# Expert and attention kernel: early weight loads into later homes, and key features summed on VectorE

## The chip, the cores and the metric

The kernel runs on one core of a Trainium2 chip. A core has five engines that each follow a queue of their own: TensorE (PE; its weight loads are listed as PEld), VectorE (DVE), ScalarE (ACT), GpSimd (POOL) and SyncE (SP), which here issues DMAs. The metric is the device time of one execution in microseconds (us). Three runs of the kernel before were timed.

## The reference

Three stages follow one another: linear attention over 4 batches of 576 tokens and 8 heads, a gated product of four weight matrices, and a routing to one of 8 experts for each token.

```
def phi(x):
    proj = einsum('bhsd,df->bhsf', x, w_phi)             # 64 -> 128 features
    proj = proj - max(abs(proj), axis=-1, keepdims=True)
    return concatenate([exp(proj), exp(-proj)], axis=-1)
q_p, k_p = phi(q), phi(k)
kv  = einsum('bhsf,bhsd->bhfd', k_p, v)
z   = sum(k_p, axis=2)                                  # key features, summed over a batch's tokens
num = einsum('bhsf,bhfd->bhsd', q_p, kv)
den = einsum('bhsf,bhf->bhs', q_p, z)[..., None] + 1e-06
x   = (num / den), heads side by side                    # 2304 x 512
x   = ((x @ w1) * (x @ w2) @ w3) @ w_out                 # 512 -> 1024 -> 1024 -> 512, float64 weights
...
out[mask] = gate_w[mask, None] * (relu(x[mask] @ ew1[e]) @ ew2[e])   # for each expert e
```

The weights w1, w2, w3 and w_out of the middle stage arrive as float64, and are turned into float32 on the chip.

## The kernel before, in words

**Precision.** Most products run in three passes on a split of each operand into a high and a low part (mm3: high by high, high by low, low by high; lines 118 to 120). The split is a copy of the high part (line 102 on ScalarE, 104 on VectorE) and a subtraction (line 110, on VectorE or GpSimd). Products on plain float32 operands ("native") show two records for each instruction.

**Start of the program.** The start stage runs from the first load to the first product with w1 (tile pab). It does two things side by side. One is batch 0 of the attention. The other is the preparation of the weights: 40 blocks of 512 KB of float64 (8 of w_out, 8 of w1, 8 of w2, 16 of w3) are loaded as integers (tile raw, three buffers, line 207, 235 or 277) and converted by three VectorE instructions (lines 130, 132, 134, in f64_to_f32; the result is y, or wo for w_out). A block of w1 or w2 is then split into w1h and w1l, or w2h and w2l (ScalarE, and GpSimd for the low part). A block of w_out is transposed (tile pt), copied to woT and multiplied with the expert embeddings (tile pl); when all 8 are done, the last columns of wo are filled in (wo_c). Two blocks of w3 make one of 8 column blocks of W' = w3 @ w_out: 8 products each (tile pw, line 283), then a split of the two PSUM tiles into wph and wpl. PSUM gives 3 banks to pw, pab and px (tag pm) and 5 to the attention and the w_out work (tag pa).

**Attention.** Key and query tiles are 128 tokens by 4 heads (a group g; two groups make the 8 heads). A batch has 576 tokens, four whole tiles and a half one, which two batches share; so a batch is five pieces in each group. For one key piece the unit phi loads the tile (qkraw) and the values (v, two buffers), makes the projection (pphi), the largest absolute value (mx, line 325, VectorE) and eight exponentials on ScalarE into two tiles kf (lines 338 and 339; three buffers). The unit kv then issues four products with the values (kv, line 373) and four with a tile of ones, 32 columns wide (kz, line 377), which gives the sum z. After the fifth piece both PSUM tiles are copied (kvs), transposed (pkv, pkz) and split into ch and cl by the unit fin. The query units transpose pt (pqt), take exponentials (F, Hh, Ll), multiply (po), and divide (den, xf).

**Order of the work.** TensorE executes in the order in which the program is written; the other engines follow an order chosen by a scheduler when the program is built. Each attention unit has a due time on an axis of its own (LEAD_K, KEY_T, FIN_K, GAP_K are offsets on it), and attend(t) writes all units that are due before t. In the start stage attend is called after each piece of the weight work; after that, the units stand between those of the main loop: nine blocks of 256 tokens with 8 units pab (24 products each) and 4 units px, whose order follows the due times too. Batches 1 to 3 run there. The experts follow.

Of the kernel before, what the change touches and what calls it, by code (L numbers as in the profile page):

```python
# [23 lines left out]
NF = 128  # L24
# [28 lines left out]
GAP_K = 1.5  # L53
START_T = 32.0
START_P = 0.7
# [9 lines left out]
FIN_K = 0.3  # L65
# [27 lines left out]
class Kern:  # L93
# [103 lines left out]
    def load_w12(self, sp, w1, w2, wt):  # L197

        nc = self.nc
        out = []  # L200
        for src, name in ((w1, "w1"), (w2, "w2")):
            for kc in range(4):
                for u in range(2):
                    def go(src=src, name=name, kc=kc, u=u):
                        raw = sp.tile([P, 1, 512], I64, tag="raw64", name="raw64", bufs=RAW64)
                        c = slice(u * 512, (u + 1) * 512)
# [4 lines left out]
                    out.append(go)  # L211
        return out

    def build_w(self, sp, pp, app, w3t, w_out, wph, wpl):

# [5 lines left out]
        wo = sp.tile([P, 8, 2, HB], F32, name="wo")  # L221
# [47 lines left out]
        flat = [(0.5, u) for us in units for u in us]  # L269
        for fc in range(8):  # L270
            pss = []
            for half in range(2):
                def w_unit(fc=fc, half=half, pss=pss):
                    if half == 0:
                        pss.extend(pp.tile([P, 512], F32, tag="pm", name="pw") for _ in range(2))
                    raw = sp.tile([P, 4, P], I64, tag="raw64", name="raw64", bufs=RAW64)
                    nc.sync.dma_start(out=raw, in_=w3t[half * 512:(half + 1) * 512, fc * P:(fc + 1) * P]
                                      .rearrange("(a p) f -> p a f", p=P))
                    y = self.f64_to_f32(sp, raw, [P, 4, P])
                    for u in range(2):  # L280
                        for j in range(4):
# [914 lines left out]
```

## Time and profile before

| what | us |
|---|---|
| runs | 876.34, 878.03 and 1616.35, median 878.03 |
| the profiled execution | 877.96 |
| its span, from first to last instruction | 876.2 |
| TensorE busy, share of the span | 830.4, 95% |
| VectorE busy, share | 489.5, 56% |
| ScalarE busy, share | 400.7, 46% |
| GpSimd busy, share | 238.4, 27% |

The profiled execution took 877.96 us, within 0.1 us of the median, and its span leaves 1.76 us around it. A share of busy time is an average over stages; TensorE's matmuls overlap, and their ends are modelled, so the distance between starts tells more than the length of one.

### The profile page before, as it was taken

How to read it: one execution, taken by the hardware profiler on the slowest of the kernel's cores; microseconds unless marked ns; L12 is line 12 of the kernel's file. 1: busy time of each engine (PE TensorE's matmuls, PEld its weight loads, DVE VectorE, ACT ScalarE, POOL GpSimd, SP SyncE). 2: the span in 40 equal slices, each digit the busy share in tenths (PEclk: the TensorE clock that was granted, in tenths of full speed). 3: DMA queues.
4: the chain of work that ended last, by engine and by line, in shares of the span. 5: the costliest groups of instructions: out<-in, count | busy, mean ns of one | idle time of the engine just before them, and what ended most of it. 6: DMA issues, size and time to landing. Idle time of an engine off the chain costs nothing. (4 is left out here: it accounts for less than half of the span.)

```text
span 876.2 us, 15821 instructions
## 1 busy us (share of the span) xinstructions
PE 830.4 (95%) x5986; PEld 738.0 (84%) x5986; DVE 489.5 (56%) x1130; ACT 400.7 (46%) x1073; POOL 238.4 (27%) x257
## 2 busy tenths in 40 slices
PE   6899868999999999999999999979999999999996
PEld 4577657987899987899877999979998898988974
DVE  5788896653479844588543795443475362432200
ACT  5543335455576557475555763313243452433211
POOL 1122344321255312254212542130013301201010
PEclk9999988999999999999999999999999999999999
DMA  6677532002101011111011000032316641522410
GB/s 208 223 225 220 161 109 76 19 25 66 50 26 43 14 56 49 50 37 32 25 55 44 25 25 1 26 98 79 85 38 211 193 145 43 186 91 76 166 41 15
DMA packets 63536, 73.45 MB, mean 84 GB/s; under 512 B 7832, under 2 KB 50072, under 8 KB 63458
## 3 DMA queue, kind: packets, MB, share of 16 engines
q1 hardware_dynamic: 59618, 62.68, 23.1%
q0 software_dynamic: 3680, 9.72, 3.2%
q8 instruction: 48, 0.79, 0.4%
q14 instruction: 30, 0.25, 0.1%
q10 hardware_dynamic: 160, 0.02, 0.0%
HBM read 61.71 MB, written 10.95 MB: 83 GB/s over the span
## 5 line engine op out<-in xcount | busy, mean ns | idle before, releaser
L110 POOL TENSOR_TENSOR Ll<-F,Hh 128x512 fp32r<-128x512 f32 (+1 forms) x64 | 93.3, 1457 | 107.5 <-ACT Hh L102 101.2
L118 PE MATMUL px<-wph,abh 128*128 128x260 f32 x288 | 83.4, 290 | 5.0 <-DVE abh L104 5.0
L118 PE MATMUL pab<-xh,w1h 128*128 128x256 f32 x288 | 84.9, 295 | 0.1
L120 PE MATMUL pab<-xh,w1l 128*128 128x256 f32 x288 | 82.4, 286 | 0.0
L119 PE MATMUL pab<-xl,w1h 128*128 128x256 f32 x288 | 82.3, 286 | 0.0
L118 PE MATMUL pab<-xh,w2h 128*128 128x256 f32 x288 | 82.2, 285 | 0.0
L119 PE MATMUL pab<-xl,w2h 128*128 128x256 f32 x288 | 82.1, 285 | 0.0
L120 PE MATMUL px<-wph,abl 128*128 128x260 f32 x288 | 82.1, 285 | 0.0
L119 PE MATMUL px<-wpl,abh 128*128 128x260 f32 x288 | 82.1, 285 | 0.0
L120 PE MATMUL pab<-xh,w2l 128*128 128x256 f32 x288 | 82.0, 285 | 0.0
L567 DVE TENSOR_TENSOR ab<-pab,a 128x256 f32<-128x256 f32 x72 | 30.5, 423 | 89.5 <-ACT a L565 89.1
L119 PE MATMUL ph<-xsl,wth 128*128 128x256 f32 (+1 forms) x256 | 75.7, 296 | 0.5 <-DVE xsl L110 0.5
L118 PE MATMUL ph<-xsh,wth 128*128 128x256 f32 (+1 forms) x256 | 75.9, 296 | 0.3 <-ACT xsh L102 0.3
L120 PE MATMUL ph<-xsh,wtl 128*128 128x256 f32 (+1 forms) x256 | 75.5, 295 | 0.0
L565 ACT COPY a<-pab 128x256 f32<-128x256 f32 x72 | 27.0, 375 | 103.1 <-PE pab L120 87.7
L522 DVE RECIPROCAL den<-den 128x256 f32<-128x256 f32 (+1 forms) x32 | 62.3, 1948 | 16.2 <-ACT den L517 16.2
L283 PE MATMUL pw<-wo,y 128*128 128x260 f32 x256 | 62.7, 399 | 8.9 <-DVE wpl L110 7.5
L110 POOL TENSOR_TENSOR qkl<-qkraw,qkh 128x256 fp32r<-128x256 f32 x52 | 38.5, 743 | 114.9 <-ACT qkh L102 97.2
L283 PEld LDWEIGHTS pw<-wo,y 128*128 128x128 f32 x256 | 49.8, 199 | 19.2 <-DVE wpl L110 8.7
L901 DVE SCALAR_TENSOR_TENSOR hh<-ph,hh 128x256 fp32r<-128x256 f32 (+1 forms) x96 | 31.1, 353 | 58.0 <-ACT hh L897 49.5
L118 PEld LDWEIGHTS px<-wph,abh 128*128 128x128 f32 x288 | 55.0, 191 | 8.8 <-DVE abh L104 5.5
L829 POOL DMA_INDIRECT out_dram<-ob,ids x20 | 20.5, 1026 | 139.0 <-ACT ob L919 118.8
(220 smaller groups left out, 2390.6 us busy)
## 6 DMA issues: line engine op xcount, KB each, us to landing
wraw<-in_moe_w_dram SPq DMA_DIRECT2D x32, 512.0 KB
raw<-in_moe_w_dram SPq DMA_DIRECT2D x16, 512.0 KB
raw<-in_moe_w3t_dram SPq DMA_DIRECT2D x16, 512.0 KB
v<-in_v_dram SPq DMA_DIRECT2D x40, 128.0 KB
qkraw<-in_kT_dram SPq DMA_DIRECT2D x36, 128.0 KB
qkraw<-in_qT_dram SPq DMA_DIRECT2D x36, 128.0 KB
x2d<-x SPq DMA_DIRECT2D x18, 256.0 KB
raw<-in_moe_w_out_dram SPq DMA_DIRECT2D x8, 512.0 KB
```

Source lines behind the costliest of these rows:

```text
L110: e.tensor_tensor(out=out, in0=a, in1=b, op=ALU.subtract)
L118: nc.tensor.matmul(out, lhsT=lh, rhs=rh, start=start, stop=False)
L119: nc.tensor.matmul(out, lhsT=lh, rhs=rl, start=False, stop=False)
L120: nc.tensor.matmul(out, lhsT=ll, rhs=rh, start=False, stop=stop)
L283: nc.tensor.matmul(pss[u][:, :HB], lhsT=y[:, j, :], rhs=wo[:, jc, u, :], start=jc == 0, stop=jc == 7)
L522: nc.vector.reciprocal(den[:, :n], den[:, :n])
L565: nc.scalar.copy(a, ps[:, :BLK])
L567: nc.vector.tensor_tensor(out=ab, in0=ps[:, BLK:], in1=a, op=ALU.mult)
L829: self.nc.gpsimd.indirect_dma_start(out=out, out_offset=IndirectOffsetOnAxis(ap=ids[:m, i, 0:1], axis=0), in_=ob[:m, :], in_offset=None, b ...
L901: nc.vector.scalar_tensor_tensor(out=lo(h, i, j), in0=x, scalar=0.0, in1=h[:, i:j].bitcast(F32), op0=ALU.max, op1=ALU.subtract)
```

## The change

**Loads.** The raw blocks of w_out and w1 no longer go through the three buffers of raw. Each has a place of its own (tiles rwo and rw): in the memory that w2h, w2l, wph and wpl take later. Their loads are issued ahead, in pairs of w_out and w1, five ahead of the work (LOOK). w2 and w3 still go through raw, with each load issued three units ahead. All 8 blocks of w1 are converted beside the 8 of w_out; then come 8 groups of one block of w2 and two of w3. Attention units up to time 14 (START_K) stand in the first part, the rest up to 32 in the second; before, a power of the weight work's share set this.

**Key sums.** The first whole piece of a group writes its features into two tiles kacc (KACC = 2 buffers, so one group's worth). The other four pieces are added to them by VectorE, two instructions each, on 64 partitions for a half piece. The four products with ones run once a group, on kacc (unit sums, SUM_K after the last piece), so kz holds a PSUM bank only then. fin comes later (FIN_K), and a gap after a batch's keys is longer (GAP_K). kv_split writes ch and cl in four smaller splits for each pair of heads in place of two.

```diff
@@ -50,9 +50,10 @@
-GAP_K = 1.5
+GAP_K = 2.0
-START_P = 0.7
+START_K = 14.0
+LOOK = 5
-FIN_K = 0.3
+FIN_K = 1.0
+SUM_K = 0.1
+KACC = 2
...
-    def load_w12(self, sp, w1, w2, wt):
+    def early_raw(self, base, w1, w_out):
+        self.raw_wo, self.raw_w1, loads = [], [], [[], []]
+        for x, tag, n, name, dst in ((w_out, "w2h", 4 * DM, "rwo0", self.raw_wo), (w_out, "w2l", 4 * DM, "rwo1", self.raw_wo),
+                                     (w1, "wph", 4 * (BLK + 4) * 2, "rw10", self.raw_w1),
+                                     (w1, "wpl", 4 * (BLK + 4) * 2, "rw11", self.raw_w1)):
+            t = base.tile([P, n], I64, tag=tag, name=name, bufs=1)
+            for a in range(4):
+                i = len(dst)
+                raw = t[:, a * 512:(a + 1) * 512]
+                r, c = (i, slice(0, DM)) if x is w_out else (i // 2, slice((i % 2) * 512, (i % 2 + 1) * 512))
+                dst.append(raw.rearrange("p (a b) -> p a b", a=1))
+                loads[x is w1].append(lambda raw=raw, x=x, r=r, c=c:
+                                      nc.sync.dma_start(out=raw, in_=x[r * P:(r + 1) * P, c]))
+        return [x for pair in zip(*loads) for x in pair]
+
+    def conv_w1(self, sp, i, wt):
+        y = self.f64_to_f32(sp, self.raw_w1[i], [P, 1, 512])
+        c = slice((i % 2) * 512, (i % 2 + 1) * 512)
+        self.split(wt["w1h"][:, i // 2, c], wt["w1l"][:, i // 2, c], y[:, 0, :], WHI, WLO)
+
+    def late_w(self, sp, pp, base, w2, w3t, wt):
...
-        for src, name in ((w1, "w1"), (w2, "w2")):
-                    def go(src=src, name=name, kc=kc, u=u):
-                        nc.sync.dma_start(out=raw[:, 0, :], in_=src[kc * P:(kc + 1) * P, c])
-                        y = self.f64_to_f32(sp, raw, [P, 1, 512])
-                        self.split(wt[name + "h"][:, kc, c], wt[name + "l"][:, kc, c], y[:, 0, :], WHI, WLO)
...
+            def load():
+                st["r"] = sp.tile(shape, I64, tag="raw64", name="raw64", bufs=RAW64)
+                nc.sync.dma_start(out=st["r"] if shape[1] > 1 else st["r"][:, 0, :], in_=src)
+
+            out.append((load, lambda: unit(self.f64_to_f32(sp, st["r"], shape))))
...
+        def w2_unit(y, i):
+            if i == 0:
+                for n in ("w2h", "w2l"):
+                    wt[n] = base.tile([P, 4, DF], F32R, tag=n, name=n, bufs=1)
...
+            if fc == 0:
+                wp[:] = [base.tile([P, 8, 2, HB], F32R, tag=n, name=n, bufs=1) for n in ("wph", "wpl")]
+            for u in range(2):
+                self.split(wp[0][:, fc, u, :], wp[1][:, fc, u, :], pss[u][:, :HB], "a", "v")
+        for fc in range(8):
+            piece(w2[fc // 2 * P:(fc // 2 + 1) * P, (fc % 2) * 512:(fc % 2 + 1) * 512], [P, 1, 512],
+                  lambda y, fc=fc: w2_unit(y, fc))
+            for half in range(2):
+                piece(w3t[half * 512:(half + 1) * 512, fc * P:(fc + 1) * P].rearrange("(a p) f -> p a f", p=P), [P, 4, P],
+                      lambda y, fc=fc, half=half: w_unit(y, fc, half))
...
-                raw = sp.tile([P, 1, DM], I64, tag="raw64", name="raw64", bufs=RAW64)
-                nc.sync.dma_start(out=raw[:, 0, :], in_=w_out[jc * P:(jc + 1) * P, :])
+                raw = self.raw_wo[jc]
...
-            kf = ap.tile([P, 2, 256], F32, tag="kfk" if keep else "kf", name="kf", bufs=4 if keep else KB_)
+            tag, bufs = kind
+            kf = ap.tile([P, 2, 256], F32, tag=tag, name=tag, bufs=bufs)
...
+    def key_sums(self, zp, acc):
-            self.nc.tensor.matmul(out(zp, 32 * h, 32, 0), lhsT=self.one32[r0:r1, :],
-                                  rhs=kfs[h // 2][r0:r1, :, (h % 2) * NF:(h % 2 + 1) * NF], start=first, stop=last)
+            self.nc.tensor.matmul(zp[32 * h:32 * h + 32, 0:256].rearrange("p (s f) -> p s f", s=2), lhsT=self.one32,
+                                  rhs=acc[h // 2][:, :, (h % 2) * NF:(h % 2 + 1) * NF], start=True, stop=True)
...
-        so = pz[:, :256].rearrange("p (s h x) -> p h s x", h=4, x=32)[:, 2 * r:2 * r + 2, :, 0:1]
-        so = so.to_broadcast([P, 2, 2, D])
-        self.split(val(ch), val(cl), sv, CHI[self.ph], CLO[self.ph])
-        self.split(one(ch), one(cl), so, CHI[self.ph], CLO[self.ph])
+        so = pz[:, :256].rearrange("p (s h x) -> p h s x", h=4, x=32)
+        for c in range(2):
+            h, l = (x[:, c * 256:(c + 1) * 256].rearrange("p (s y d) -> p s y d", s=2, y=2) for x in (ch, cl))
+            self.split(h[:, :, c, :], l[:, :, c, :], sv[:, c], CHI[self.ph], CLO[self.ph])
+            self.split(h[:, :, 1 - c, :], l[:, :, 1 - c, :], so[:, 2 * r + c, :, 0:1].to_broadcast([P, 2, D]),
+                       CHI[self.ph], CLO[self.ph])
...
-                    st["f"] = self.key_feats(*self.phi_tile("k", t, g), keep)
+
+                    kind = ("kfk", 4) if keep else ("kacc", KACC) if n == whole else ("kf", KB_)
...
-                        kvp[:] = [self.app.tile([P, 512], F32, tag="pa", name=x) for x in ("kv", "kz")]
+                        kvp[0] = self.app.tile([P, 512], F32, tag="pa", name="kv")
-                    self.kv_native(*kvp, st["v"], st["f"], r0, r1, n == 0, n == len(pieces) - 1)
+                    last = n == len(pieces) - 1
+                    self.kv_native(kvp[0], st["v"], st["f"], r0, r1, n == 0, last)
+                    todo = [(st["f"], r0, r1)]
+                    if n == whole:
+
+                        todo = [(self.kept[g], *pieces[0][1:])] if whole else []
+                        acc[:] = st["f"]
+                    for f, a, e in todo if n >= whole else ():
+                        for r in range(2):
+                            nc.vector.tensor_tensor(out=acc[r][a:e], in0=acc[r][a:e], in1=f[r][a:e], op=ALU.add)
...
+                def sums(kvp=kvp, acc=acc):
+                    kz = self.app.tile([P, 512], F32, tag="pa", name="kz")
+                    self.key_sums(kz, acc)
+                    x = self.ap.tile([P, 320], F32, tag="xf", name="kvs1", bufs=1)
+                    nc.scalar.copy(x[:, :256], kz[:, :256])
+                    kvp[1] = x
...
+            out.append((time + SUM_K, sums))
...
-    wt = {n: base.tile([P, 4, DF], F32R, name=n) for n in ("w1h", "w1l", "w2h", "w2l")}
-    wph = base.tile([P, 8, 2, BLK + 4], F32R, name="wph")
-    wpl = base.tile([P, 8, 2, BLK + 4], F32R, name="wpl")
+    wt = {n: base.tile([P, 4, DF], F32R, name=n) for n in ("w1h", "w1l")}
+    k.wp = []
...
+        loads = k.early_raw(base, w1, w_out)
         attend(START_0)
-        lw = k.load_w12(sp, w1, w2, wt)
-        wu = k.build_w(sp, pm, papool, w3t, w_out, wph, wpl)
-        for c, u in wu:
+        for i, us in enumerate(wou):
+            ahead(2 * i + LOOK)
+            if i == len(wou) - 1:
+                for x in range(RAW64):
+                    late_w[x][0]()
+            for u in us:
+                u()
+            if i < 8:
+                k.conv_w1(sp, i, wt)
+            attend(START_K * (i + 1) / len(wou))
+        for i, (_, u) in enumerate(late_w):
-            done += c
-            while lw and n - len(lw) < n * done / tot:
-                lw.pop(0)()
-            attend(START_T * (done / tot) ** START_P)
+            if i + RAW64 < len(late_w):
+                late_w[i + RAW64][0]()
+            attend(START_K + (START_T - START_K) * (i + 1) / len(late_w))
```

TensorE, start of the program, before: the end of the w_out work (pt and pl), the first products for W' (pw), and the keys of the second group (each piece is pphi, kv and kz).

```order
L316 MATMUL pphi<-bd,qkraw 128x256 x2
L251 MATMUL pl<-woT,enT 8x128 x8
L373 MATMUL kv<-kf,v_106 64x256 x4
L377 MATMUL kz<-kf,one_108 32x256 x4
L264 MATMUL pt<-ident,ls 128x8 x8
L283 MATMUL pw<-wo,y_482 128x260 x8
L316 MATMUL pphi<-bd,qkraw 128x256 x2
L443 MATMUL pkv<-ident,kvs_464 128x128 x4
L443 MATMUL pkz<-ident,kvs_466 128x128 x2
L373 MATMUL kv<-kf,v_107 64x256 x4
L377 MATMUL kz<-kf,one_108 32x256 x4
L283 MATMUL pw<-wo,y_554 128x260 x8
```

TensorE after the change, from the same place in the keys (the last pieces of the first group):

```order
L305 MATMUL pl<-woT,enT 8x128 x4
L348 MATMUL pphi<-bd,qkraw 128x256 x2
L405 MATMUL kv<-kfk,v_102 64x256 x4
L294 MATMUL pt<-ident,wo 128x128 x4
L305 MATMUL pl<-woT,enT 8x128 x4
L348 MATMUL pphi<-bd,qkraw 128x256 x2
L411 MATMUL kz<-kacc,one_104 32x256 x4
L294 MATMUL pt<-ident,wo 128x128 x4
L305 MATMUL pl<-woT,enT 8x128 x4
L405 MATMUL kv<-kacc,v_103 64x256 x4
L491 MATMUL pkv<-ident,kvs_428 128x128 x4
L491 MATMUL pkz<-ident,kvs_476 128x128 x2
```

The first pw stands behind eight key pieces in place of five and behind the first group's transposes (pkv, pkz), and kz follows once after a group; kv on kacc stands three rows behind kz.

VectorE, start of the program, before: conversions of w_out (wo) and w1 (y), and the largest absolute values mx.

```order
L130 TENSOR_SCALAR wo<-raw_234 128x2x256
L132 SCALAR_TENSOR_TENSOR wo<-raw_234,wo 128x2x256
L130 TENSOR_SCALAR y_202<-raw_200 128x512
L325 TENSOR_REDUCE mx<-pphi 128x4
L132 SCALAR_TENSOR_TENSOR y_202<-raw_200,y_202 128x512
L134 SCALAR_TENSOR_TENSOR wo<-raw_234,wo 128x2x256
L134 SCALAR_TENSOR_TENSOR y_202<-raw_200,y_202 128x512
L130 TENSOR_SCALAR wo<-raw_259 128x2x256
L132 SCALAR_TENSOR_TENSOR wo<-raw_259,wo 128x2x256
L134 SCALAR_TENSOR_TENSOR wo<-raw_259,wo 128x2x256
```

VectorE after the change, at the same place:

```order
L133 TENSOR_SCALAR wo<-rwo_133 128x2x256
L135 SCALAR_TENSOR_TENSOR wo<-rwo_133,wo 128x2x256
L469 TENSOR_TENSOR kacc<-kacc,kf 128x512
L133 TENSOR_SCALAR y_204<-rw_135 128x512
L137 SCALAR_TENSOR_TENSOR wo<-rwo_133,wo 128x2x256
L135 SCALAR_TENSOR_TENSOR y_204<-rw_135,y_204 128x512
L469 TENSOR_TENSOR kacc<-kacc,kf 128x512
L137 SCALAR_TENSOR_TENSOR y_204<-rw_135,y_204 128x512
L133 TENSOR_SCALAR y_227<-rw_135 128x512
L133 TENSOR_SCALAR wo<-rwo_133 128x2x256
L135 SCALAR_TENSOR_TENSOR y_227<-rw_135,y_227 128x512
L135 SCALAR_TENSOR_TENSOR wo<-rwo_133,wo 128x2x256
```

The additions into kacc stand between the conversions, and conversions of w1 come one for each of w_out; before, three stood beside the eight of w_out.

TensorE, batch 2, in the main loop, end of the first group's keys, after the change (pphi in three passes is a later key tile):

```order
L405 MATMUL kv<-kfk,v_102 64x256 x4
L121 MATMUL pphi<-bd_h,qkh 128x256
L122 MATMUL pphi<-bd_l,qkh 128x256
L123 MATMUL pphi<-bd_h,qkl 128x256
L121 MATMUL pphi<-bd_h,qkh 128x256
L122 MATMUL pphi<-bd_l,qkh 128x256
L123 MATMUL pphi<-bd_h,qkl 128x256
L411 MATMUL kz<-kacc,one_104 32x256 x4
L405 MATMUL kv<-kacc,v_103 64x256 x4
L121 MATMUL pab<-xh_73,w1h 128x256
```

The products of the next group with kacc stand directly behind kz; before, kz of the last piece was followed by six pphi and the six transposes pkv and pkz, and the features of the next group had buffers of their own.

## Rows read from the trace of the kernel before

**Rows 1.** The page, part 1: busy time, share of the span, instructions.

```profile
PE 830.4 (95%) x5986; PEld 738.0 (84%) x5986; DVE 489.5 (56%) x1130; ACT 400.7 (46%) x1073; POOL 238.4 (27%) x257
```

**Rows 2.** Windows: length; busy us (instructions) of PE, PEld, DVE, ACT, POOL; clock; DMA; GB/s.

```profile
0.00:8.40 8.40, 3.35 (x8) 2.51 (x8) 1.78 (x7) 2.85 (x7) 2.32 (x16) 1.00 0.60 177
0.00:42.80 42.80, 31.55 (x212) 19.72 (x212) 27.19 (x54) 24.32 (x75) 6.99 (x19) 0.96 0.69 220
42.80:88.00 45.20, 45.08 (x251) 34.09 (x252) 36.86 (x65) 17.87 (x58) 9.81 (x8) 1.00 0.70 218
88.00:152.40 64.40, 49.23 (x239) 41.77 (x238) 52.67 (x78) 28.47 (x68) 28.81 (x25) 0.91 0.37 116
152.40:580.00 427.60, 422.33 (x3498) 387.20 (x3498) 263.37 (x628) 235.81 (x669) 143.05 (x156) 0.99 0.12 34
175.00:242.00 67.00, 65.76 (x557) 54.35 (x557) 28.46 (x68) 36.14 (x119) 15.97 (x21) 1.00 0.16 46
```

**Rows 3.** Waits of TensorE, 0 to 154 us: total, times, longest.

```profile
PE pw L283 <- DVE wpl L110: 7.5, 2, 3.9
...
PE po L118 <- DVE xf L526: 3.6, 1, 3.6
...
PE pt L240 <- ACT kf L339: 2.1, 1, 2.1
```

**Rows 4.** Waits of TensorE, 158 to 500 us, the longest.

```profile
PE pphi L118 <- ACT kf L339: 2.2, 2, 1.1
```

**Rows 5.** Order in time on TensorE (start, length): products of one key piece, then pw.

```profile
60.69 1.08 PE L373 MATMUL kv<-kf,v 128*64 128x256 f32 x8
61.70 0.64 PE L377 MATMUL kz<-kf,one 128*32 128x256 f32 x8
62.27 3.77 PE L283 MATMUL pw<-wo,y 128*128 128x260 f32 x16
```

**Rows 6.** TensorE in time, main loop: kz, then px.

```profile
200.76 0.64 PE L377 MATMUL kz<-kf,one 128*32 128x256 f32 x8
201.33 0.39 PE L118 MATMUL px<-wph,abh 128*128 128x260 f32 x1
```

**Rows 7.** TensorE in time: first pw, a pw after a wait, first pab.

```profile
42.85 0.46 PE L283 MATMUL pw<-wo,y 128*128 128x260 f32 x1 [1.48 <-DVE y L134]
...
92.77 3.52 PE L283 MATMUL pw<-wo,y 128*128 128x260 f32 x8 [3.93 <-DVE wpl L110]
...
152.41 0.41 PE L118 MATMUL pab<-xh,w1h 128*128 128x256 f32 x1
```

**Rows 8.** VectorE in time: the first conversion, three end to end, one beside GpSimd.

```profile
8.43 0.43 DVE L130 TENSOR_SCALAR wo<-raw 128x512 int32<-128x512 int32 x1 [0.60 <-DMA raw<-in_moe_w_out_dram]
...
32.02 0.42 DVE L130 TENSOR_SCALAR wo<-raw 128x512 int32<-128x512 int32 x1
32.35 0.68 DVE L134 SCALAR_TENSOR_TENSOR wo<-raw,wo 128x512 int32<-128x512 int32 x1
32.95 0.69 DVE L132 SCALAR_TENSOR_TENSOR wo<-raw,wo 128x512 int32<-128x512 int32 x1
...
44.03 1.46 POOL L110 TENSOR_TENSOR w1l<-y,w1h 128x512 fp32r<-128x512 f32 x1 [3.60 <-ACT w1h L102]
44.40 1.65 DVE L134 SCALAR_TENSOR_TENSOR y<-raw,y 128x512 int32<-128x512 int32 x1
```

**Rows 9.** Groups of VectorE, whole run: busy us, mean ns of one, idle before.

```profile
L110 DVE TENSOR_TENSOR wtl<-wraw,wth 128x512 fp32r<-128x512 f32 x64 | 41.1, 687 | 26.4 <-ACT wth L102 17.1 <-DMA wraw<-in_moe_w_dram 9.3
...
L110 DVE TENSOR_TENSOR cl<-pkv,ch 128x256 fp32r<-128x256 f32 x16 | 6.7, 419 | 4.8 <-ACT ch L102 4.6
```

**Rows 10.** ScalarE in time: first and eighth exponentials of a key piece.

```profile
51.26 0.35 ACT L338 ACTIVATE kf<-pphi,mx 128x128 f32<-128x128 f32 x1
...
53.01 0.41 ACT L339 ACTIVATE kf<-pphi,mn 128x128 f32<-128x128 f32 x1
```

**Rows 11.** Window in which the weight loads run at their densest.

```profile
8.00:10.00 2.00, 2.00 (x7) 0.95 (x7) 1.53 (x4) 2.00 (x9) 0.00 (x0) 1.00 1.04 346
```

More of the change, by code (lines that the diff above doesn't have):

```diff
@@ new lines, in conv_w1, with piece, w_unit @@
+    def conv_w1(self, sp, i, wt):
[3 more added lines that the diff above has]
+    def late_w(self, sp, pp, base, w2, w3t, wt):
+        nc = self.nc
+        HB = BLK + 4
+        out = []
+        wp = self.wp
+        def piece(src, shape, unit):
+            st = {}
+            def load():
[6 more added lines that the diff above has]
+                    wt[n] = base.tile([P, 4, DF], F32R, tag=n, name=n, bufs=1)
+            c = slice((i % 2) * 512, (i % 2 + 1) * 512)
+            self.split(wt["w2h"][:, i // 2, c], wt["w2l"][:, i // 2, c], y[:, 0, :], WHI, WLO)
+        pss = []
+        def w_unit(y, fc, half):
+            if half == 0:
+                pss[:] = [pp.tile([P, 512], F32, tag="pm", name="pw") for _ in range(2)]
+            for u in range(2):
+                for j in range(4):
+                    jc = 4 * half + j
+                    nc.tensor.matmul(pss[u][:, :HB], lhsT=y[:, j, :], rhs=self.wo[:, jc, u, :],
+                                     start=jc == 0, stop=jc == 7)
+            if half == 0:
+                return
+            if fc == 0:
+                wp[:] = [base.tile([P, 8, 2, HB], F32R, tag=n, name=n, bufs=1) for n in ("wph", "wpl")]
+            for u in range(2):
+                self.split(wp[0][:, fc, u, :], wp[1][:, fc, u, :], pss[u][:, :HB], "a", "v")
[5 more added lines that the diff above has]
+                      lambda y, fc=fc, half=half: w_unit(y, fc, half))
@@ L220, in build_w @@
         half = {}
-        wo = sp.tile([P, 8, 2, HB], F32, name="wo")
+        wo = self.wo = sp.tile([P, 8, 2, HB], F32, name="wo")
         def en_t():
@@ L268, in build_w @@
         units[9].append(wo_c)
[L269 to L281, printed above, removed]
-                            jc = 4 * half + j
-                            nc.tensor.matmul(pss[u][:, :HB], lhsT=y[:, j, :], rhs=wo[:, jc, u, :],
-                                             start=jc == 0, stop=jc == 7)
-                    if half == 0:
-                        return
-                    for u in range(2):
-                        self.split(wph[:, fc, u, :], wpl[:, fc, u, :], pss[u][:, :HB], "a", "v")
-                flat.append((3.1, w_unit))
-        return flat
+        return units
     def attn_init(self, ap, app, sp, qT, kT, vv):
@@ L326, in phi_tile, with key_feats @@
         return p3, m
-    def key_feats(self, p3, m, keep):
+    def key_feats(self, p3, m, kind):
         nc, ap = self.nc, self.ap
@@ L363, in load_v, with kv_native @@
         return v
-    def kv_native(self, kvp, zp, v, kfs, r0, r1, first, last):
+    def kv_native(self, kvp, v, kfs, r0, r1, first, last):
         def out(x, q, n, a):
@@ L404, in key_units, with phi @@
         pieces = self.pieces(b)
+        whole = int(pieces[0][1] > 0)
         for g in range(2):
             kvp = [None, None]
+            acc = []
             for n, (t, r0, r1) in enumerate(pieces):
                 st = {}
[L410 removed]
+                def phi(st=st, t=t, n=n, g=g, r0=r0, r1=r1, whole=whole):
                     self.ph = int(b > 0)
```

40 lines of the change are left out of this document (18 added, 22 removed).

## The prediction

> **What bounds the kernel now.** First the page: TensorE is busy for 95% of the span, the next engine for 56% [rows 1]. An average hides stages, so next the windows, cut at the places that the order in time shows: the first product for W' (pw) at 42.85 us and the first product with w1 (pab) at 152.41 us [rows 7]. After 152.4 us TensorE is all but full, 422.3 of 427.6 us [rows 2], and its longest wait between 158 and 500 us is 2.2 us in two pieces [rows 4]. There a microsecond of TensorE work is a microsecond of time. The start stage is another kind. Up to 42.8 us TensorE has 31.6 us of work, then 45.1 of 45.2, then 49.2 of 64.4, so it is idle for 11.2 + 0.1 + 15.2 us. VectorE is busy for 27.2, 36.9 and 52.7 us of the same stretches [rows 2]. The waits name it: pw for a PSUM bank that VectorE frees (7.5 us in two), po for xf (3.6 us) [rows 3]. In the last third the conversions and the division queue up on VectorE while TensorE stands; in the middle third it is the other way round.
>
> **Removed: products with ones.** Five pieces, two groups and four batches make 40 sets of four kz before, and 8 after. A set costs TensorE the distance from its start to the next instruction: 62.27 - 61.70 = 0.57 us [rows 5], and 201.33 - 200.76 = 0.57 us in the main loop [rows 6]. Its busy length, 0.64, overlaps the next. 24 of the 32 removed sets lie in the main loop: 24 x 0.57 = 13.7 us, on the path. The other 8 lie in the start stage: 4.6 us of TensorE work, on the path only where VectorE isn't.
>
> **Added: additions on VectorE.** Four pieces x two instructions x 8 groups are 64, 16 in each batch. The trace has no such addition; the nearest row is a subtraction of two SBUF tiles of 128x512, 0.687 us [rows 9], and set end to end instructions of that length start 0.60 us apart (32.35 to 32.95 [rows 8]). Beside GpSimd one of 0.69 took 1.65 us [rows 8]. So 0.60 to 1.65; I take 0.65, since most stand alone. In the key stage of the main loop (175 to 242 us) VectorE is busy for 28.5 of 67 us [rows 2]; 10.4 us more, or even 26, leaves it unfilled, so these cost nothing. Without that cover 48 x 0.65 = 31 us would be at stake. In the start stage 16 x 0.65 = 10.4 us come on the engine that is late.
>
> The pair of rows at the end of that group is also where a rule speaks against the change. The Trainium skill (SBUF — State Buffer, section "SBUF: two separate sides") says that VectorE with two SBUF inputs and GpSimd with an SBUF input take turns on a shared port pair, each holding it for a whole instruction. The trace agrees as far as 1.65 beside 0.69 goes. By it every addition could lose up to a GpSimd instruction (1.46 us); in the start stage that would be up to 16 x 1.46 = 23 us on VectorE by that page, in place of what I take.
>
> **Smaller splits.** Each group's split is 8 ScalarE and 8 VectorE instructions of half the size in place of 4 of 0.42 [rows 9]. Bounds for a half-size one: 0.21 (if time goes with size) and 0.42 (if it doesn't); I take 0.26, so 0.4 us more a group on each engine (0 to 1.7), covered in the main loop as the additions are. The two waits in front of them, SUM_K and FIN_K, come later by under 1 on the due axis, with other products in between.
>
> **A new wait: kacc has buffers for one group only.** So the next group's first whole piece must wait on ScalarE until kz has been read. Behind it stand ScalarE's copies for pab and TensorE's kv. Eight exponentials start 0.25 us apart [rows 10]: 2.0 us, plus 0.41 for the last. In batches 1 and 3 some 5 us of products stand between kz and that kv, so nothing is lost. In batch 2 kv follows kz directly: about 2.8 us until it is done in place of 1.0 (60.69 to 61.70 [rows 5]), so 1.8 us lost. In batch 0 the same stands in a stretch with idle time. The additions of the last piece, 2 x 0.65, have to end before kz; a key tile's projection and often a pab unit stand between, so I take 0, with 1 us for each of six groups as the upper bound. Main loop: -13.7 + 1.8 = **-11.9 us** (-13.7 to -6).
>
> **The start stage, first part.** The first pw needs conversion 12 of VectorE before the change; after it, number 18 (16 of w_out and w1, one of w2, one of w3). A conversion is three instructions: 0.60 + 0.33 + 0.60 = 1.53 us packed (a start to the next, 32.02 to 32.95, and the third at 0.60) [rows 8], up to 1.8 when each waits for the one before; I take 1.65. To the 27.2 us that VectorE is busy up to 42.8 [rows 2] come 6 conversions (9.9), three mx (1.8, at 0.60), 12 additions (7.8) and one group's small splits (2): 48.7 us. VectorE starts its first conversion at 8.43 us [rows 8], with 1.8 us done by then [rows 2], so without a gap pw starts at 8.4 + 46.9 = **55 us**, 12 us later than now. The loads can keep up: 19 blocks of 0.52 MB with keys and values of 2.6 MB are 12.6 MB, 36 us at the 346 GB/s seen at the densest [rows 11] and 57 us at the mean of 220 [rows 2]. I take the first, since loads now queue without waiting for a buffer; by the second the first part would end some 5 us later.
>
> What early loads can spoil: the third key tile is issued behind seven 512 KB blocks and a values tile that waits for the first kv. At 346 GB/s seven blocks take 10.6 us, so it lands at about 17 us. Conversions of the blocks that have landed cover that, so it costs nothing; without the cover it would be 4 or 5 us once. The Trainium skill (DMA: Bandwidth & Descriptors, section "Queues, rings and completion order") has each ring consume its descriptors in order, which is the reason for "behind".
>
> **The start stage, second part.** From 42.85 to 152.4 us TensorE is busy for 94.3 us [rows 2]. Part of that is the lower of its two clock levels, 1.2 in place of 2.4 GHz, after a wait: half a unit of pw took 3.52 us at 92.77 [rows 7], against 1.9 (half of 3.77 [rows 5]). The mean clock of 0.91 in the last third makes it at most 0.09 x 64.4 = 5.8 us [rows 2]; I take 5.5, which leaves 89 us of plain work. Three key pieces' projections (3 x 1.0) and kv (3 x 1.0), one group's transposes (0.75) and four sets of kz (2.3) leave it: 80 us. VectorE is busy for 89.6 us there and loses 6 conversions (11, at a mean between plain and disturbed ones), three mx, and a group's splits, and gains four additions: about 78 us. So the load of the two is even throughout, where before TensorE was full in the middle third and VectorE late in the last. The 15.3 us of waits and 5.5 of low clock go to between 6 and 21; I take 12. So pab starts at 55 + 80 + 12 = **147 us**, 5.4 earlier (141 to 156).
>
> **Sum.** 876.2 - 5.4 - 11.9 = 858.9 us of span, and with the 1.76 us around it 860.7; **861 us**, 1.9% under the median of 878.03. That is next to the 2% (860.5) that a measurement of this kernel can tell from no change, so the forecast's own range, 855 to 867, lies on both sides.
>
> **Rivals.**
> *The start stage runs without stalls.* For it: TensorE has 80 and VectorE 78 us of work after pw, spread evenly, and one PSUM bank more is free while keys run (kz held it; a wait of 2.1 us for it is in [rows 3]). Against it: VectorE's last third has the divisions. Waits of 4: pab at 139, main loop -13.7: 876.2 - 13.4 - 13.7 + 1.8 + 1.76 = 853.
> *The early loads bring nothing.* The first part gets 12 us longer because conversions, not loads, hold it up, and the second part keeps its waits: 55 + 80 + 20 = 155, +2.6. 876.2 + 2.6 - 11.9 + 1.76 = 869.
> *Key sums become a wait at each group.* Six groups in the main loop each lose 2.3 us between the last features, VectorE's turn and kz; that is all of 13.7. 876.2 - 5.4 - 13.7 + 13.7 + 1.76 = 873. Against it: VectorE's room in that stage.
> *Slower: additions beside GpSimd.* If additions in the start stage cost 1.65 in place of 0.65, the 12 before pw delay it by 12 us, to 67, and the rest keeps its 21 us of waits: pab at 168, +15.6; total 876.2 + 15.6 - 11.9 + 1.76 = 882. It decides from pab at 164.3 us on. Against it: GpSimd is busy for 7 of the first 43 us [rows 2]; its eight w1l add some 7 us.
>
> **How the numbers follow.** Forecast 0.40, no stalls 0.22, early loads nothing 0.20, a wait at each group 0.13, slower 0.05. The range leaves out the last and half of the edges: 849 to 874. Faster by over 2%: half of the forecast, all of the first rival and a little: 0.44; within 2%: 0.51; slower by over 2% needs 895.6 us, beyond any sum here: 0.05.
>
> **What would show it.** In the trace after: kz starts 8 times in place of 40, each still 0.57 to the next instruction; pw starts at 53 to 58 us, with VectorE nearly full from 8 us on; pab at 141 to 156; from pab to the end about 12 us less than the 723.8 of now. In batch 2 TensorE waits for an exponential behind kz, 1 to 2.5 us, and in no other batch of the main loop. VectorE's share rises by about 40 us. Wrong it would be if kz waits for kacc additions in the main loop, if pw starts after 60, or if the low clock takes more of the start stage than the 5.5 us of now, since TensorE has more idle time ahead of pw.

## The result and the profile after

The changed kernel takes 868.26 us, median of four executions (867.16 to 868.66), against 877.18 for the kernel before, timed beside it: a ratio of 0.9898, 95% interval 0.9881 to 0.9914. One execution of the kernel before, at 1616 us, lies far from its others (876.06 to 878.03) and is left out of the ratio. The profiled execution took 867.16 us, 6 more than forecast. The gain of 10.8 us of span is made of two parts of opposite sign, which the windows show. They are cut at the first pw and the first pab, as those of before in [rows 2]; a row has the stretch and its length, then busy time of PE, PEld, DVE, ACT and POOL with the instructions, the granted clock, the DMA share and GB/s.

```profile
8.40:65.70 57.30, 37.91 (x218) 22.28 (x216) 49.51 (x88) 32.64 (x111) 17.17 (x9) 0.88 0.61 208
65.70:156.00 90.30, 82.47 (x415) 68.98 (x416) 73.73 (x126) 35.43 (x92) 30.08 (x26) 0.97 0.47 148
156.00:865.40 709.40, 692.72 (x5095) 638.70 (x5093) 405.75 (x1006) 330.17 (x897) 193.94 (x207) 0.99 0.21 66
```

The third row is the gain: 709.4 us from pab to the end in place of 723.8, 14.4 less. The first two are the start stage: it ends 3.6 us later than before (156.0 against 152.4), and 9 later than forecast. The first part is at fault, 57.3 us from 8.4 on where 46.9 was forecast. The second part took 90.3 where 92 was forecast and 109.6 was measured before. VectorE is idle for 7.8 us of the first row (57.30 less 49.51), and TensorE stands at a mean granted clock of 0.88 there. What VectorE waits for in that row (total us, times, longest) is five short waits of different origin, and loads are 1.4 us of it (the first of their two waits began before the row):

```profile
DVE kacc L469 <- ACT kf L372: 2.7, 3, 2.2
DVE y L133 <- PE pl L305: 1.6, 2, 1.2
DVE wo L133 <- DMA rwo<-in_moe_w_out_dram: 1.4, 2, 0.8
DVE cl L113 <- ACT ch L105: 1.2, 2, 0.9
DVE y L133 <- POOL w1l L113: 1.2, 1, 1.2
```

The page's shares moved as forecast, VectorE by 41.3 us (from the 489.5 of [rows 1]):

```profile
PE 816.3 (94%) x5730; PEld 732.2 (85%) x5730; DVE 530.8 (61%) x1226; ACT 400.9 (46%) x1105; POOL 243.5 (28%) x257
```

TensorE's waits up to pab, which answer to [rows 3] (us in total, times, longest):

```profile
PE pt L294 <- DVE wo L137: 7.9, 3, 4.1
PE pphi L348 <- DMA qkraw<-in_kT_dram: 5.6, 2, 5.2
PE pw L253 <- DVE y L137: 4.1, 1, 4.1
PE pw L253 <- DVE wpl L113: 3.1, 2, 1.6
```

The waits of the second part have shrunk (wpl from 7.5 to 3.1 us). The new ones, for wo and y, are the first part's conversions. The chronological view of TensorE has the two marks of the start stage, as in [rows 7], and in batch 2 the set of kz with what follows it (start, length, instruction, and in brackets the idle time ahead of it):

```profile
65.69 4.52 PE L253 MATMUL pw<-wo,y 128*128 128x260 f32 x12 [4.09 <-DVE y L137]
...
156.04 0.41 PE L121 MATMUL pab<-xh,w1h 128*128 128x256 f32 x1
...
332.26 0.64 PE L411 MATMUL kz<-kacc,one 128*32 128x256 f32 x8
333.61 2.19 PE L405 MATMUL kv<-kacc,v 128*64 128x256 f32 x8 [0.71 <-ACT kacc L372]
335.74 0.39 PE L121 MATMUL pab<-xh,w1h 128*128 128x256 f32 x1
...
356.49 0.64 PE L411 MATMUL kz<-kacc,one 128*32 128x256 f32 x8
357.06 0.66 PE L491 MATMUL pkv<-ident,kvs 128*128 128x128 f32 x4
```

A set of kz still costs 0.57 us to the next instruction (356.49 to 357.06). Behind the one at 332.26 kv waits for the exponentials of kacc, the wait that the prediction named for batch 2; kv itself then takes 2.13 us to the next instruction, in place of 1.01 in [rows 5], at a granted clock of 1.00. ScalarE's eight exponentials of kacc run from 332.94 to 335.11 beside it, so its products follow one pair after the other:

```profile
333.60:335.80 2.20, 2.19 (x9) 0.83 (x9) 0.00 (x0) 2.20 (x11) 0.00 (x0) 1.00 0.20 60
```

In the first part the same wait shows on three engines. First VectorE:

```profile
46.65 0.68 DVE L135 SCALAR_TENSOR_TENSOR y<-rw,y 128x512 int32<-128x512 int32 x1
47.25 0.68 DVE L357 TENSOR_REDUCE mx<-pphi 128x4 f32<-128x512 f32 x1
47.85 0.68 DVE L137 SCALAR_TENSOR_TENSOR y<-rw,y 128x512 int32<-128x512 int32 x1
50.73 0.72 DVE L469 TENSOR_TENSOR kacc<-kacc,kf 128x512 f32<-128x512 f32 x1 [2.20 <-ACT kf L372]
```

Then ScalarE and TensorE:

```profile
46.89 0.37 ACT L371 ACTIVATE kacc<-pphi,mx 128x128 f32<-128x128 f32 x1 [1.96 <-PE kz L411]
...
46.22 0.64 PE L411 MATMUL kz<-kacc,one 128*32 128x256 f32 x8
...
49.11 1.08 PE L405 MATMUL kv<-kacc,v 128*64 128x256 f32 x8 [0.64 <-ACT kacc L372]
51.78 0.97 PE L491 MATMUL pkv<-ident,kvs 128*128 128x128 f32 x4 [1.59 <-ACT kf L372]
```

ScalarE may not write the second group's kacc until kz has read the first group's. Eight exponentials later kv starts, four more later (49.51 to 50.70) the addition, and behind that addition VectorE's conversions stand for 2.2 us.

### The profile page after: what moved, and what is told of

It is laid out like the page before. It is cut to its first block, busy times and chain, and to the rows that moved or that the text cites. A ratio compares the mean times of both kernels' runs of the same rounds, so it can differ in the third digit from the quotient of the medians.

```text
span 865.4 us, 15433 instructions
## 1 busy us (share of the span) xinstructions
PE 816.3 (94%) x5730; PEld 732.2 (85%) x5730; DVE 530.8 (61%) x1226; ACT 400.9 (46%) x1105; POOL 243.5 (28%) x257
## 5 line engine op out<-in xcount | busy, mean ns | idle before, releaser
L123 PE MATMUL px<-wph,abl 128*128 128x260 f32 x288 | 82.5, 287 | 0.0
L122 PE MATMUL px<-wpl,abh 128*128 128x260 f32 x288 | 82.5, 286 | 0.0
L571 DVE RECIPROCAL den<-den 128x256 f32<-128x256 f32 (+1 forms) x32 | 62.3, 1947 | 9.2 <-ACT den L566 9.1
```

Of the source, the lines that this page charges most:

```text
L122: nc.tensor.matmul(out, lhsT=lh, rhs=rl, start=False, stop=False)
L123: nc.tensor.matmul(out, lhsT=ll, rhs=rh, start=False, stop=stop)
L571: nc.vector.reciprocal(den[:, :n], den[:, :n])
```

## Experiments

All were set against the kernel before, on the same chip within a group (1 to 4, 5 to 8, 9 to 12). Times of pw and pab are first starts in us; from pab to the end is the span less pab.

| run | pw | pab | pab to end | median | ratio, 95% interval |
|---|---|---|---|---|---|
| before | 42.85 | 152.4 | 723.8 | 875 to 877 | 1 |
| changed | 65.7 | 156.0 | 709.4 | 868.26 | 0.9898, 0.9881 to 0.9914 |
| 1 loads only | 60.4 | 158.3 | 718.3 | 878.44 | 1.0042, 1.0017 to 1.0068 |
| 2 sums only | 44.3 | 153.2 | 709.8 | 865.16 | 0.9875, 0.9842 to 0.9908 |
| 3 products in batch 0 | 60.7 | 153.8 | 707.7 | 864.41 | 0.9876, 0.9831 to 0.9921 |
| 4 fewer keys first | 57.1 | 150.7 | 707.4 | 861.18 | 0.9842, 0.9810 to 0.9874 |
| 5 own home for kacc | 62.3 | 152.2 | 710.6 | 864.77 | 0.9886, 0.9869 to 0.9903 |
| 6 additions doubled | 65.3 | 155.8 | 715.0 | 872.50 | 0.9961, 0.9940 to 0.9982 |
| 7 w1 low by ScalarE | 64.0 | 154.5 | 709.3 | 864.74 | 0.9880, 0.9863 to 0.9897 |
| 8 products, fewer keys | 54.2 | 149.2 | 710.0 | 861.60 | 0.9861, 0.9833 to 0.9888 |
| 9 changed again | 66.6 | 157.1 | 708.1 | 866.57 | 0.9896, 0.9865 to 0.9926 |
| 10 fewer keys, own home | 56.4 | 153.3 | 707.8 | 863.28 | 0.9859, 0.9829 to 0.9888 |
| 11 loads, fewer keys | 55.2 | 148.6 | 720.0 | 871.85 | 0.9946, 0.9922 to 0.9971 |
| 12 still fewer keys | 54.7 | 157.5 | 706.4 | 865.26 | 0.9878, 0.9849 to 0.9908 |

The changed kernel was profiled twice (9): pab differs by 1.1 us and the rest by 1.3, so differences of that size say nothing. All ratios lie within 2% of 1; two times are called different below only where their intervals don't overlap.

**1 and 2, each part alone.** In 1 the functions from key_feats to key_units and their constants are those of before, in 2 they alone are those of the changed kernel.

```diff
 # 1, on the changed kernel
-GAP_K = 2.0
+GAP_K = 1.5
...
-            out.append((time + SUM_K, sums))
+                        kvp[:] = [self.app.tile([P, 512], F32, tag="pa", name=x) for x in ("kv", "kz")]
...
```

> The early loads and the new order of the start stage, with the ones products of every piece as before (40 sets of kz, no additions, the full-size splits, the old gaps on the due axis). Theory A (additions on VectorE are what made the first part 10 us longer than forecast: 12 of them at about 0.7 us, and VectorE standing behind them until the exponentials are done): the first pw starts at 54 to 58 us in place of 65.7, the first pab at 146 to 152, the main loop stays as in the kernel before (about 724 us from pab to the end), and the time is 870 to 876. Rival B (the early loads and their conversions are what takes the time): the first pw stays at 62 to 66 us, pab at 154 to 157, and the time is 878 to 882.

> The key sums with additions, the half-size splits and the new gaps on the due axis, with the loads and the start order of the kernel before. Both theories: 14 us less from the first pab to the end than the 724 us of before. Theory A: the additions delay this start stage as well, first pw 47 to 50 in place of 42.85, pab at 155 to 160, time 866 to 871. Rival B: the additions find room, pw at 43 to 46, pab at 150 to 153, time 861 to 864.

The loads alone are 0.4% slower, the sums alone 1.2% faster; the product of the two ratios, 0.9917, is near the 0.9898 of both. So the whole gain is the sums'. In 2 the 16 additions of batch 0 moved pab by 0.8 us only, so theory A falls there. In 1 pw comes at 60.4 us without one addition, between the two expectations, and pab at 158.3, later than either; the time is rival B's. From pab to the end it takes 718.3 us, where 724 was expected.

The 5.3 us by which pw comes earlier than in the changed kernel can't be set against the 10 us that the first part is too long: the forecast had counted 7.8 us for these additions, so by its sum pw would come at some 8.4 + 39.1 = 47.5 us here, and it comes 13 later. VectorE's work falls by 6.5 us (49.51 to 43.06), but it is now idle for 8.9, and the longest of its waits is one for TensorE's projection (the window up to pw, then the wait):

```profile
8.40:60.40 52.00, 39.13 (x273) 22.00 (x271) 43.06 (x69) 30.94 (x103) 11.02 (x8) 0.93 0.63 216
...
DVE mx L355 <- PE pphi L346: 5.3, 4, 2.5
```

**3, the additions out of batch 0.**

```diff
+                    if b == 0:
+                        todo = []
+                        for h in range(4):
+                            nc.tensor.matmul(kvp[1][32 * h:32 * h + 32, 0:256].rearrange("p (s f) -> p s f", s=2),
+                                             lhsT=self.one32[r0:r1, :],
...
+                                             start=n == 0, stop=last)
...
```

> The changed kernel, but batch 0 sums its keys with products with ones at each piece as before; the additions stay in batches 1 to 3. Theory A: the 12 additions before pw are gone, pw starts at 54 to 58 us, pab at 148 to 152, main loop as in the changed kernel (709 us), time 860 to 864. Rival B: pw at 62 to 66, pab at 155 to 157, time 867 to 869.

pw moved by 5.0 us, as in 1, and pab by 2.2 (3.3 against the second profile of the changed kernel, 9). pw and pab lie between the two expectations, the time just above A's range. As in 1, the wait for kacc is gone too, and VectorE waits for pphi in its place (4.3 us in two).

**4, 12 and 10, how many key pieces stand ahead of pw.** START_K is 9 in 4 and 10 and 6 in 12, in place of 14.

```diff
-START_K = 14.0
+START_K = 9.0
```

> The changed kernel with 9 in place of 14 on the due axis as the point that the key units reach before the first pw (about what the order of the kernel before had), so fewer key pieces and additions ahead of pw. Theory A: pw starts at 55 to 60 us, but the additions only move behind it, into the stretch where VectorE has 75 of 90 us of work, so pab is at 153 to 157 and the time 865 to 869. Rival C (the key work ahead of pw, whatever engine does it, leaves TensorE idle and in low clock): pab at 147 to 151, time 859 to 863.

> The changed kernel with 6 in place of 14 on the due axis ahead of pw. Theory K (fewer key pieces ahead of pw start the stretch with full TensorE sooner): pw at 51 to 54, pab at 148 to 151, time 857 to 861. Rival (the point is reached: with 9 TensorE already had no wait between 60 and 100 us, so what leaves the first part only fills the second): pab at 150 to 153, time 860 to 864.

> The changed kernel with both changes that helped: 9 in place of 14 on the due axis ahead of pw, and a home of its own for the second group's kacc in batch 0. Theory (the two take out the same wait: with fewer keys ahead of pw the second group's exponentials come behind it, where ScalarE waits only 1.1 us for kz): no further gain over fewer keys alone, pw at 56 to 58, pab at 149.5 to 151, time 859 to 862. Rival (they add up, 3.8 and 5.3 us): pab at 146 to 148, time 856 to 859.

With 9, six sets of kv stand ahead of pw in place of eight, VectorE is idle for 4.3 us, and pab comes 5.3 us earlier, as rival C had it. It has the lowest median of all, 1.6% under the kernel before, with an interval that lies below that of the changed kernel's first timing and overlaps that of its second (9), as well as those of 2, 8 and 10. Its first part:

```profile
8.40:57.10 48.70, 34.08 (x186) 19.21 (x185) 44.38 (x74) 25.17 (x78) 16.58 (x9) 0.86 0.67 232
```

With 6, four sets of kv stand ahead of pw; it comes 2.4 us earlier still, and pab 6.8 later:

```profile
8.40:54.70 46.30, 26.59 (x154) 15.71 (x153) 41.16 (x68) 21.85 (x64) 14.60 (x9) 0.84 0.65 229
54.70:157.50 102.80, 96.70 (x478) 77.52 (x479) 81.21 (x145) 48.04 (x138) 29.50 (x27) 0.93 0.45 144
```

TensorE has 26.6 us of work in the 46.3 ahead of pw, and its second part then holds 96.7. So fewer keys no longer help, against theory K of this run, and the point that the rival named was not only reached but passed: pab and the time (157.5 and 865.26 us) are later than the rival had them. 10 adds nothing to 4, as its theory had it, but its pab, 153.3, and its time, 863.28, are above the theory's ranges too, pab 2.6 us later than in 4; no run here says why.

**11, the loads without sums, with fewer keys.** Run 1 with START_K = 9.

> The early loads with the products with ones of every piece as before (no additions anywhere), and 9 in place of 14 on the due axis ahead of pw. Theory K (what made the early loads alone slower, 158.3 in place of 152.4 at pab, was the order that puts eight key pieces ahead of pw, not the loads): pw at 53 to 55, pab at 149 to 153, time 869 to 874. Rival L (the conversions that have to come ahead of pw are the loss, whatever the order): pw at 57 or later, pab at 155 to 158, time 876 to 879.

pab at 148.6 us: theory K, with pw and pab 0.2 and 0.4 us outside its ranges. The same early loads cost 0.4% with eight key pieces ahead of pw and bring 0.5% with six. Beside the sums their gain is not shown: 4 and 2, with and without the early loads, differ by 0.3%, and their intervals overlap. Why 1 takes 97.9 us in its second part, with one wait of 4.7 us of po for pt on VectorE, where the changed kernel takes 90.3 for nearly the same work of TensorE (84.8 us against 82.5), was not followed up.

**5, the wait for kacc.** The second group of batch 0 gets a kacc in the memory that xl0 takes later.

```diff
+    kx = base.tile([P, 2, 2, 256], F32, tag="xl0", name="kaccx", bufs=1)
...
-            kf = ap.tile([P, 2, 256], F32, tag=tag, name=tag, bufs=bufs)
+            kf = own[r] if own else ap.tile([P, 2, 256], F32, tag=tag, name=tag, bufs=bufs)
```

> The changed kernel, but in batch 0 the second group's kacc has a home of its own, so its exponentials no longer wait on ScalarE until kz has been read. Theory D (that wait, put at nothing in the prediction for batch 0, is what leaves VectorE idle ahead of pw: in the changed kernel ScalarE waits 2.0 us for kz at 46.9 us, and VectorE 2.2 us for the exponentials at 50.7): the first pw starts at 61 to 63.5 us in place of 65.7, pab at 152 to 154, time 864 to 866. Rival A (VectorE's 49.5 us of work ahead of pw sets it, and the idle time only moves to another wait): pw at 64.5 to 66.5, pab at 155 to 157, time 867 to 869.

Theory D in the start stage: pw 3.4 us earlier, pab 3.8. The windows show VectorE almost without a gap ahead of pw (3.0 us idle in place of 7.8), and a second part of the same length as in the changed kernel:

```profile
8.40:62.30 53.90, 37.88 (x217) 22.23 (x215) 50.91 (x88) 32.64 (x110) 18.23 (x9) 0.87 0.66 222
62.30:152.20 89.90, 83.36 (x415) 69.72 (x416) 74.04 (x126) 35.90 (x92) 30.79 (x26) 0.96 0.47 149
```

The ratios of 5 and of the changed kernel overlap; 5 takes 1.2 us more after pab, which is no more than two profiles of one kernel differ by. The gain is shown in the trace, not in the time.

**6, the cover of the main loop.**

```diff
+                            if b:
+                                nc.vector.tensor_tensor(out=acc[r][a:e], in0=acc[r][a:e], in1=f[r][a:e], op=ALU.max)
```

> The changed kernel with a second instruction of the same size behind each addition in batches 1 to 3 (a maximum of the sum and the summand, which leaves the sum as it is): 48 more on VectorE, about 31 us. The prediction's claim, that the main loop covers them: from pab to the end 709 to 712 us as against 709.4, time 867 to 871. Rival (a wait at each group: kz comes later by the 1.3 us that the last piece's second pair takes, or pab's conversions queue up behind them): 6 x 1.3 = 8 us or more, time 875 to 885.

Neither expectation holds: 715.0 us after pab, 5.6 more than in the changed kernel, and 872.50 us, between the two ranges. Cut at the last product with w1 (the changed kernel, then this one):

```profile
156.00:612.30 456.30, 448.43 (x3604) 420.89 (x3603) 315.11 (x758) 247.41 (x720) 152.40 (x166) 0.99 0.14 42
...
612.30:865.40 253.10, 244.29 (x1494) 217.81 (x1492) 90.64 (x249) 82.76 (x177) 41.54 (x41) 0.99 0.34 109
```

```profile
155.80:615.00 459.20, 450.00 (x3604) 419.65 (x3603) 342.00 (x806) 248.32 (x720) 156.84 (x166) 0.99 0.14 41
615.00:870.80 255.80, 245.75 (x1494) 219.32 (x1492) 90.79 (x249) 82.86 (x177) 40.95 (x41) 0.98 0.35 108
```

48 instructions and 27 us more on VectorE cost 2.9 us where they stand, about a tenth; TensorE's waits have a new row there, kv for kf, 1.8 us in four, which would follow if the additions hold kf's buffers longer (not shown). The other 2.7 us lie behind the last such product, where nothing was changed: a wait of ph for xsh, 1.4 us in place of 0.3, and 1.4 more TensorE time, which run 5 has too.

**7, GpSimd off VectorE's back.**

```diff
-        self.split(wt["w1h"][:, i // 2, c], wt["w1l"][:, i // 2, c], y[:, 0, :], WHI, WLO)
+        for n in ("w1h", "w1l"):
+            nc = self.nc
+            nc.scalar.copy(wt[n][:, i // 2, c], y[:, 0, :])
```

> The changed kernel, but the low part of w1 is not subtracted by GpSimd: ScalarE writes a plain copy in its place (the low part of w1 is left out, the values are not those of the reference). GpSimd is then nearly idle ahead of pw, and ScalarE has 8 copies of 0.6 us more. Theory P (VectorE loses time beside GpSimd: instructions of 0.69 us took 1.64 at 20.19, two additions 2.84 at 30.75, one of 0.43 took 1.06 at 39.42, two of them 1.82 at 61.92; and 1.2 us of waiting for the low part's buffer): VectorE's busy time ahead of pw falls by 3 to 6 us, pw starts at 60 to 62.5, pab at 151 to 154, time 862 to 866. Rival A: pw at 64 to 67, because ScalarE's extra copies take back what VectorE gains; time 867 to 870.

```profile
8.40:64.00 55.60, 37.42 (x217) 22.26 (x216) 45.01 (x87) 37.07 (x120) 1.59 (x1) 0.88 0.62 215
```

VectorE's busy time falls by 4.5 us (49.51 to 45.01). One conversion instruction of some 0.6 us has moved out of the window (87 in place of 88), so GpSimd's work cost VectorE about 3.9 us: 1.5 on the 12 additions (9.68 to 8.15 us), the rest on the conversions. But its idle time rises from 7.8 to 10.6, with 4.1 us of waiting for the exponentials ahead of additions, and pw gains 1.7 us. Busy time and time are theory P's, pw is rival A's, pab (154.5) lies between: most of what VectorE gains it gives back waiting. ScalarE, with the extra copies, is busy for 4.4 us more there (37.07 against 32.64), so the run shows what GpSimd's work costs VectorE, but not what it costs the time.

**8 and 9, the sum of two, and the changed kernel again.**

> The changed kernel with products with ones in batch 0 and 9 in place of 14 on the due axis ahead of pw. If the two parts of the VectorE load ahead of pw (additions, key pieces) each cost what they did alone (5.0 and 8.6 us of pw, 2.2 and 5.3 of pab), pw starts at 53 to 55 us, pab at 148 to 150, time 857 to 861. Rival: VectorE is no longer what is late once one of the two is gone (in the run with fewer keys TensorE had no wait for it between 60 and 100 us), pab stays at 150 to 153 and the time at 860 to 864.

> The changed kernel as it is, beside the next three on the same chip, so that they can be set against it directly. Every theory: a ratio to the kernel before of 0.987 to 0.993, first pw at 65 to 66.5, first pab at 155 to 157.

pw and pab of 8 add up in part (54.2 and 149.2 us), but the time is that of 4: the rest is 2.6 us longer there, and the ratios overlap. 9 gives the ratio that was expected; pw and pab come 0.1 us after the expected ranges.

## Why the prediction was right where it was, and wrong where it was not

**The time** came out 7 us above the forecast, inside its range, but by two misses of opposite sign: the start stage ended 9.0 us later than forecast, and the rest took 2.5 us less.

**Main loop: right in the mechanism, beyond the range in size.** -11.9 us forecast (-13.7 to -6), -14.4 measured. TensorE has 191 instructions fewer from pab to the end (5286 to 5095), which is 24 sets of 8 less one record, and its busy time falls by 11.8. Half of the other 2.6 is px's wait at the end of the loop, 5.0 us in the kernel before and 3.7 in the changed one. That wait is 3.1 in both runs without sums too, and their time after pab is 5.5 (1) and 3.8 us (11) shorter than before. The forecast had no such term, and what makes it up beyond the shorter wait is open. With the loads alike the sums bring 8.9 (1 to the changed kernel) and 12.6 us (11 to 4), with the old loads 14.0 (2). So the sums' own part lies about the forecast, and by the pairs with like loads it is the missing term that carries the total beyond the range.

**The wait in batch 2: right in sum.** The forecast had 2.8 us from the set of kz to the end of kv, in place of 1.0. It is 2.91 (332.26 + 0.57 to 335.74), of which the list of waits shows only the 0.71 ahead of kv.

**Additions covered: nearly.** No kz waits for an addition, which was named as a sign of being wrong. Run 6 puts a second set at 2.9 us where "these cost nothing" stood; what the first 48 cost was not measured apart.

**Second part: right.** 80 + 12 = 92 us forecast, 90.3 measured. TensorE is busy for 82.5 us, of which the lower clock is 2.7 at most, and idle for 7.8: the load is even, and half of the waits are gone, as the prediction had it against "the early loads bring nothing". That rival's pab, 155, and its 869 us came out, but by another way: the second part gained, the first lost more.

**First part: wrong, by 10.4 us** (57.3 from 8.4 us on, against 46.9). The step that failed is "without a gap pw starts at 8.4 + 46.9", together with "In batch 0 the same stands in a stretch with idle time". VectorE's work is 2.6 us more than summed (49.5 against 46.9), and 7.8 us are gaps (7.8 in the second profile of the changed kernel too), which the sum put at nothing. The idle time that the prediction relied on is TensorE's; the engine that is late is VectorE, and it stood behind an addition that waited for exponentials that waited for kz. Run 5 takes that wait out: pw comes 3.4 us earlier, with 4.8 us less of idle time and 1.4 more of work. The other gaps are the short waits of VectorE's list in the section on the result. Gaps don't come with the additions alone: without any, run 1 has 8.9 us of them, of other origin.

The work is the smaller term, and run 7 shows where it comes from: about 3.9 us beside GpSimd's subtractions. The price of 1.65 for a conversion held a little of that, and "since most stand alone" was right of most additions: by their lengths the 12 took 1.5 us more than without GpSimd, far from the 12 us of the rival "slower". So the conversions beside w1l were priced too low.

**Loads: right.** They were no limit of the first part, although its length, 57.3 us, is what the prediction gave for the mean of 220 GB/s. VectorE waited for loads for 1.4 us in all, and the third key tile was there at 18.3 us, where 17 was forecast. (The 346 GB/s of [rows 11] is not the densest stretch of 2 us in the kernel before: from 22 to 24 us it moved 359.)

**What the forecast didn't weigh** is that the first part's content is a choice. Eight key pieces ahead of pw were taken as given; runs 4, 11 and 12 show that their number moves pab by up to 10 us (148.6 in 11, 158.3 in 1) and decides whether the early loads cost or bring time.

The signs named in the prediction: kz 8 times, VectorE +41 us, pab to the end, and batch 2 hold. pw after 60 was a sign of being wrong, and was one. So was the lower clock: reckoned as the prediction did, by what the mean granted clock lacks of 1, it takes at most 0.12 x 57.3 + 0.03 x 90.3 = 9.6 us of the start stage, more than the 5.5 named (7.5 for the whole start stage before, reckoned alike). 6.9 of it lie ahead of pw, where TensorE is idle for 19 us anyway.

## What to carry to other kernels

When work is moved onto the engine that is late, price the chain that it joins, not its busy time alone: an in-order queue stands behind an instruction whose inputs come by way of two other engines, and a buffer count of one group puts a third into the chain. A sum of busy times without gaps is a lower bound; of the 10.4 us that it missed here, 7.8 were waits and 2.6 more work on VectorE than summed, by run 7 contention. Taking one wait out (5) or the added work (1, 3) gave back a third to a half of that, since the next wait took its place. And when a change has two parts, run each alone: here one was the whole gain, and the other, alone, cost time until one number of the order was set anew (14 to 9: 1.0042 and 0.9946 of the time before).

## What the hardware showed that was not expected

VectorE and GpSimd lose time on both sides. In the first part of the changed kernel two additions took 2.84 us, set end to end, where two of 0.69 take 1.28 in run 4, while GpSimd's subtraction took 3.13 in place of 1.27 (VectorE's row, that of run 4, then GpSimd's):

```profile
30.75 2.84 DVE L469 TENSOR_TENSOR kacc<-kacc,kf 128x512 f32<-128x512 f32 x2
...
29.62 1.28 DVE L469 TENSOR_TENSOR kacc<-kacc,kf 128x512 f32<-128x512 f32 x2
...
28.24 3.13 POOL L113 TENSOR_TENSOR w1l<-y,w1h 128x512 fp32r<-128x512 f32 x1 [5.28 <-ACT w1h L105]
31.64 1.41 POOL L113 TENSOR_TENSOR w1l<-y,w1h 128x512 fp32r<-128x512 f32 x1 [0.27 <-ACT w1h L105]
...
57.38 1.27 POOL L113 TENSOR_TENSOR w1l<-y,w1h 128x512 fp32r<-128x512 f32 x1 [6.48 <-ACT w1h L105]
```

The Trainium skill (SBUF — State Buffer, section "SBUF: two separate sides") has VectorE with two SBUF inputs and GpSimd take turns on a shared port pair; rows and run 7 agree. The upper bound that the prediction drew from it, a GpSimd instruction of 1.46 us for each of 16 additions, is 17.5 us for the 12 ahead of pw, over four times what the whole first part lost by run 7 (3.9).

A long wait of TensorE costs more than its length, as the prediction had it for pw in [rows 7]. After 3.65 us of px's wait its products start 0.22 us apart, where 0.12 is usual, which is the lower of the two clock levels (1.2 in place of 2.4 GHz), for 5.8 us, until 584.2. Behind the 0.71 us wait of kv in batch 2 the granted clock stayed at 1.00. In run 4, behind px's wait of 3.26 us, the slow products last 3.5 us. The last row is the window, with a granted clock of 0.50:

```profile
578.38 0.58 PE L121 MATMUL px<-wph,abh 128*128 128x260 f32 x1 [3.65 <-DVE abh L107]
...
583.78 0.42 PE L121 MATMUL px<-wph,abh 128*128 128x260 f32 x1
584.00 0.42 PE L122 MATMUL px<-wpl,abh 128*128 128x260 f32 x1
584.22 0.39 PE L123 MATMUL px<-wph,abl 128*128 128x260 f32 x1
584.43 0.29 PE L121 MATMUL px<-wph,abh 128*128 128x260 f32 x1
584.56 0.28 PE L122 MATMUL px<-wpl,abh 128*128 128x260 f32 x1
...
578.40:584.40 6.00, 6.00 (x26) 5.75 (x27) 2.90 (x7) 1.60 (x4) 0.71 (x1) 0.50 0.51 156
```
